# Recurrent attention with a routed expert layer: identities written by ScalarE, the elimination's first step a copy, and another order of the steps

## The chip, the cores and the metric

The kernel runs on one core of one Trainium2 chip. The metric is the device time of one execution in microseconds (us). Five engines work side by side, each through its own list of instructions in a fixed order: TensorE (PE; its weight loads are shown as PEld), VectorE (DVE), ScalarE (ACT), GpSimd (POOL) and SyncE (SP), which issues most of the transfers.

## What is computed

For each of 4 x 8 pairs of batch and head a state of 40 x 40 runs through 768 steps; its outputs are the rows that a layer of eight experts then takes:

```
for t in range(S):
    y[:, :, t] = einsum('bhd,bhde->bhe', rt, state)
    Sa = einsum('bhde,bhe->bhd', state, at)
    state = state * wt[:, :, None, :] - einsum('bhd,bhe->bhde', Sa, bt) + einsum('bhd,bhe->bhde', vt, kt)
x = y.transpose(0, 2, 1, 3).reshape(B * S, H * D)
...
out[i] = gate_w[i] * (relu(x[i] @ w1[e]) @ w2[e])      # e = argmax(x[i] @ w_gate), up to capacity rows an expert
```

## The kernel before

The sequence is cut into six tiles of 128 steps (index i), each of two chunks of 64 (c); two pairs of batches (pr) are worked side by side. For every tile: the decays are scanned and multiplied in (`scan_g`, `scan_p`, `mul_a`, `mul_kb`, VectorE); products of a and k or b go to PSUM (`kk`, `nn`, `iden`, TensorE) and are taken out (`take_kk` L408, `take_nn` L413, `take_iden`); a triangular matrix of 32 x 32 blocks is inverted on VectorE, and its blocks joined by TensorE and ScalarE (`inverse` L451); then the state goes through the chunks (`chain` L591), and the finished tile is gated and routed (`gate` L772, `route`). After the last tile the experts run (`expert` L1219, `weights` L1172), TensorE's matmuls mostly.

The inverse. `begin2` (L557) transposes `ns` into `xu`, one instruction of VectorE at L559. `nu` begins as 32 x 32 identities in each of 128 partitions: `units` (L553) takes the one `nu` buffer and `unit_` (L455) writes it on GpSimd, a memset (L457) and an affine select (L458). `elim(s)` (L470) then runs for s = 0 to 30 (to 14 in the first tile, where `nb` is 2): a multiply into `tmp` (L474), an add into `nu` (L476), each needing the one before. `back_a` (L481, instruction L483) and `back_b` (L485, L488) transpose the result back. There is one `ns`, one `xu` and one `nu`, so a tile's inverse begins after the previous one is joined: `take_a` (L531) of the second pair gives back `ns` and `nu`, `take_b` (L546) `xu`. `take_nn` writes `ns` (L54) and so stands ahead of `begin2`.

The masks. `masked` (L308) writes a product with its upper part zeroed, in one of two ways: ScalarE copies it out of PSUM (L311) and GpSimd selects in place, one half of the partitions after the other (L313); or VectorE multiplies it by a mask straight from PSUM (L317). `take_kk` uses it for `tm` (128 x 512), `take_m` (L703) for `vu` (128 x 1024), 24 times each.

The order. No step is issued where it stands in the code. `steps` (L67) records each with the engines and times that it is charged ("A.62 G1.5&V.35|V.69" is ScalarE 0.62 us, then GpSimd 1.5 us with VectorE held 0.35 us; or VectorE 0.69 us), its needs and its buffers. `order` (L88) replays all steps against clocks of the engines and lists them by when each could start, plus numbers by the step's name (`LATER`); of two ways it takes the one that ends first, the second with an added `alt` by kind (L182). `emit` issues the list, so every engine gets one fixed order, and an engine that waits at one instruction starts none behind it.

Of the kernel before, what the change touches and what calls it, by code (L numbers as in the profile page):

```python
# [19 lines left out]
P = 128  # L20
# [197 lines left out]
def scan_part(tc, keep, one, psum, w, a, kb, rv, vt, w_gate, wge, xd, lg, ident, up, SX, route, fill):  # L218
    nc = tc.nc
    V, A, G, TT = nc.vector, nc.scalar, nc.gpsimd, nc.tensor  # L220
# [3 lines left out]
    NQ = 2 * NI  # L224
    R = 104

    MU = 0.010321064
    O_TAIL = 0.00439068
    O_BIAS = 100
    GT = 44.0  # L230
    HC = 22.0
# [14 lines left out]
    free_ = {}  # L246
    for name, n in BUFS.items():
        sh, dt = SHAPE[name]
        pool = psum if name in ("pp", "p1") else keep if name in KEEP else one
        free_[name] = [pool.tile(sh, dt, name=f"{name}_{m}") for m in range(n)]  # L250
    LATER = {"chain": -1.1056, "comb": -0.6234, "decay": 0.0108, "decay_k": 0.6751, "fill": -93.3939,
             "gate": -0.2551, "gatf": 0.5712, "gatg": 0.0866, "h_": -87.8256, "hand_a": -95.2783,
             "hand_gx": -47.4258, "hand_kb": 32.6619, "hand_ns": -92.1286, "hand_nt": 48.4284, "hand_nu": -177.9352,
             "hand_px": -69.5935, "hand_rv": -128.1429, "hand_vT": -108.2623, "hand_vu": -1.3988,
             "hand_xu": -72.0023, "hand_z": -96.5145, "iden": -0.0389, "inverse": -0.0296, "inverse_": -116.0423,
             "join": -1.8911, "kk": 0.5138, "load_a": -8.3487, "load_g": -31.4497, "load_kb": -11.0853,
             "load_rv": -4.2772, "load_v": 3.2931, "load_w": -13.7808, "lower": -130.5284, "nn": -0.8242,
             "o_": -27.2877, "out": -0.0553, "p": 0.8687, "route": -0.5454, "routf": -1.663, "routg": -28.0939,
             "turn": -0.6375, "uT": 0.4697, "unit": -13.7726, "w": -26.1758, "w_": -0.1048, "x": -90.2429,
             "x_": -60.6701, "zz": 0.8588}  # L260
    sch = Schedule(nc, free_, MU, O_TAIL, O_BIAS, (0.549717, 1.23637, 1.47727), LATER)
    get, put, steps, PLAN, queue = sch.get, sch.put, sch.steps, sch.plan, sch.queue
    engine, copy, scale, dma = sch.engine, sch.copy, sch.scale, sch.dma

# [115 lines left out]
    def unit(T, c, G_):  # L380
# [61 lines left out]
        add(take_nn, "A.62 A.4 A.4|V.69 V.45 V.45", free=["pp"], needs=[("ns", i)], gives=("nn", n))  # L442
        add = steps(f"kk{pr}")
        add(kk, "P1.0", needs=[("a", nT), ("kb", nT)], take=["p1"])
        add(take_kk, "A.62 G1.5&V.35|V.69", take=["tm"], free=["p1"], gives=("tm", n))
        add = steps(f"iden{pr}")
        add(iden, "P.5", needs=[("kb", nT), ("nn", n), ("tm", n)], take=["pp"], free=["kb"] * c)
        add(take_iden, "A.46 A.46", take=["bk"], free=["pp"], gives=("bk", n))
# [2 lines left out]
    def inverse(i, G_, Ts):  # L451
        s_ = {}
        steps("inverse_0")(lambda: G_.update(ns=get("ns")), "", take=["ns"], gives=("ns", i))

        def unit_():  # L455
            nu = s_["nu"][:, 0:32]
            G.memset(nu, 0.0)  # L457
            G.affine_select(nu, nu, pattern=[[1, 32], [-1, 32]], compare_op=ALU.not_equal,  # L458
                            fill=1.0, base=0, channel_multiplier=0)

        nb = 2 if i in SIX else 1
        ne = 32 // nb
# [1 line left out]
        def diag(x):  # L464
            x = x.rearrange("p t s -> p (t s)")
            if nb == 1:
                return x[:, None, 0:1024].rearrange("p b (t s) -> p b t s", s=32)
            return x.rearrange("p (b y) -> p b y", b=2)[:, :, 0:512].rearrange("p b (t s) -> p b t s", s=32)

        def elim(s):  # L470
            n, m = ne - 1 - s, s + 1
            xu, nu = diag(s_["xu"]), diag(s_["nu"])
            tv = tmp[:, 0:nb * n * m].rearrange("p (b t j) -> p b t j", b=nb, t=n)
            V.tensor_mul(tv, xu[:, :, s + 1:ne, s:s + 1].to_broadcast([P, nb, n, m]),  # L474
                         nu[:, :, s:s + 1, 0:m].to_broadcast([P, nb, n, m]))
            V.tensor_add(nu[:, :, s + 1:ne, 0:m], nu[:, :, s + 1:ne, 0:m], tv)  # L476
# [81 lines left out]
            s_["xu"] = get("xu")  # L558
            V.transpose(square(s_["xu"]), G_["ns"][:, :, 0:32].rearrange("p u t -> p t u"))  # L559

        steps("unit")(units, "G2.3", take=["nu"], gives=("unit", i))
        add = steps("inverse")
        add(begin2, "V1.97", needs=[("nn", (pr, 2 * i + c)) for pr in range(2) for c in range(2)] + [("unit", i)], take=["xu"])
        for s in range(ne - 1):
            add(lambda s=s: elim(s), f"V{(nb * (ne - 1 - s) * (s + 1) + 190) / 960 * 2:.3f}")
        if nb == 1:
            add(back_a, "V1.94", gives=("ntd", 0, i))
            add(lambda: back_b(0, 1), "V1.22", gives=("n1", 0, i))
# [22 lines left out]
    def chain(T, U, Tn):  # L591
# [166 lines left out]
            more(take_turn, "A.33 A.33|V.33 V.33", take=["Sd"], free=["p1"], gives=("Sd", n))  # L758
        more = steps(f"out{pr}")
        more(mT, "P1.5", needs=[("uT", n), ("load_rv", (pr, i))], take=["pp"], free=["vT"])  # L760
        more(take_m, "A1.0 G2.6&V.7|V1.22", free=["pp"])
        more(yy, "P2.2" if q else "P1.4", needs=[("bk", n)] + [("Sd", n)] * (q > 0), take=["pp"],
             free=["bk", "vu"] + ["Sd"] * (q > 0) + ["rv"] * c)
        if q < NQ - 1:
# [7 lines left out]
    def gate(T):  # L772
        pr, i = T["pr"], T["i"]
        n = (pr, i)
        Q = {}

        def turn_y():
            p = Q["pt"] = get("pp")
            for h in range(H):
                TT.transpose(p[:, h // 4, h % 4 * P:h % 4 * P + R], T["px"][0:R, h, 0:P], ident[0:R, 0:R])  # L780

        def logits():
            p = Q["pt"]
# [12 lines left out]
        def x_lo():
            for x in range(2):
                V.tensor_sub(Q["x16"][:, x, 1, 0:HD].rearrange("p (h d) -> p h d", d=D), hv(x),
                             Q["x16"][:, x, 0, 0:HD].rearrange("p (h d) -> p h d", d=D))
            put("pp", Q["pt"])  # L800

        def x_rest():
            y = Q["x16"]
            copy(y[:, :, 1, HD:], y[:, :, 0, 2 * P:HD])
            copy(y[:, :, 0, HD:], y[:, :, 1, 2 * P:HD])

        def take_logits():
            t = pr * NI + i
            scale(lg[:, t::2 * NI, :], Q["pt"][:, 0, R:R + 16].rearrange("p (x e) -> p x e", x=2), 1.0 / SX)

        def store_x():
            for x in range(2):
                t = (pr + 2 * x) * NI + i
                dma(xd[i == NI - 1][t * P:(t + 1) * P, :], Q["x16"][:, x].rearrange("p a c -> p (a c)"))
            put("x16", Q["x16"])

        add = steps(f"gat{late(i)}{pr}")
        add(turn_y, "P1.0", needs=[("y", (pr, 2 * i)), ("y", (pr, 2 * i + 1))], take=["pp"])
        add(logits, "P1.6", needs=[("wge", 0)], free=["px"])
        add(take_logits, "A.2|V.2", gives=("logits", n))  # L820
        add(x_hi, "A.46 A.46|V.49 V.49", take=["x16"])
        add(x_lo, "V.49 V.49", free=["pp"])
        add(x_rest, "A.3 A.3|G.3 G.3")
        add(store_x, "L0>.55&L0>.55", needs=[("fill", 0)], free=["x16"], gives=("store_x", n))

    Ts = {}
# [610 lines left out]
```

## Time and profile before

| what | value |
|---|---|
| median of 3 runs | 695.71 us |
| lowest and highest run | 692.19 and 697.31 us |
| the profiled execution, its own time | 689.67 us |
| its span, from the first to the last instruction | 687.7 us |
| granted TensorE clock, mean | 0.884 |

The profiled execution is one more run with a recorder. All durations here come from it. Busy time of an engine is the time in which it executes; between two instructions that depend on each other a few tens of ns pass that count as idle. The granted clock is a share of full speed: 1.0 is 2.4 GHz, 0.5 is 1.2 GHz.

### The profile page before, as it was taken

Reading aid. Unit: us, or ns where it says so; the run is one execution under the profiler, and the core shown is the slowest. Engines: PE = TensorE matmul, PEld = TensorE weight load, DVE = VectorE, ACT = ScalarE, POOL = GpSimd, SP = SyncE. Lnnn points to the kernel's source line nnn. Section 1 sums busy time; section 2 is a strip of 40 time slices with the busy share of each in tenths; the row PEclk is TensorE's granted clock in tenths of the full one; section 3 lists DMA queues with packets and bytes.
Section 4 is the critical chain, followed back from the end, with each engine's and each line's share of the span. In section 5 each row is a group of like instructions: output and inputs, shape, how many; then the busy total and the mean of one; then the engine's idle time right before and its main releaser. Section 6 shows DMA issues by size and latency. Waiting matters only on the chain.

```text
span 687.7 us, 25344 instructions
## 1 busy us (share of the span) xinstructions
PE 559.8 (81%) x11268; PEld 438.9 (64%) x11268; DVE 444.3 (65%) x832; ACT 292.8 (43%) x569; POOL 196.8 (29%) x260
## 2 busy tenths in 40 slices
PE   0627788888878898788889866979998999999991
PEld 0626677877767788677778865736753556556471
DVE  7997899979995898798778754442424635344210
ACT  8603654535623455343553443332524534443320
POOL 8400321342222204420420024222371234241121
PEclk9955998879968987798988878979999999999997
DMA  7770043311521253034011337612789956857000
GB/s 191 209 168 4 5 108 98 102 34 55 163 83 56 80 125 95 18 97 132 27 34 37 107 103 180 151 52 67 219 157 285 217 121 173 226 118 190 24 30 13
DMA packets 72683, 74.78 MB, mean 109 GB/s; under 512 B 37644, under 2 KB 61326, under 8 KB 71604
## 3 DMA queue, kind: packets, MB, share of 16 engines
q1 hardware_dynamic: 68308, 63.08, 34.9%
q0 software_dynamic: 4256, 9.99, 5.0%
q8 instruction: 90, 1.47, 0.9%
q14 instruction: 29, 0.24, 0.1%
HBM read 57.46 MB, written 10.65 MB: 99 GB/s over the span
## 4 chain that ended last, share of the span: by engine, by line
issue 27%; PE 24%; DVE 22%; POOL 9%; ACT 7%; DMA 5%; another core or an unknown queue 2%; SPq 1%; POOLq 0%; DVEq 0%; ACTq 0%
PE pp L269 13%; DVE tmp L474 7%; DVE nu L476 7%; PE p L269 6%; POOL out_dram L1151 5%; POOL a L1124 2%; PE pp L646 2%; DVE vu L317 2%; ACT ns L54 2%; DMA px<-in_moe_w_dram 1%; DMA a<-in_a_dram 1%; POOL vT L1124 1%; PE pp L780 1%; DVE xu L559 1%
## 5 line engine op out<-in xcount | busy, mean ns | idle before, releaser
L476 DVE TENSOR_TENSOR nu<-nu,tmp 128x31 f32<-128x31 f32 (+20 forms) x170 | 69.5, 409 | 5.9
L1151 POOL DMA_INDIRECT out_dram<-tm,ri x32 | 33.1, 1035 | 133.1 <-ACT tm L1295 124.9
L474 DVE TENSOR_TENSOR tmp<-xu,nu 128x31 f32<-128x31 f32 (+20 forms) x170 | 67.4, 396 | 4.7
L313 POOL TENSOR_SCALAR_AFFINE_SELECT tm<-tm 64x512 f32<-64x512 f32 x46 | 33.1, 719 | 109.7 <-ACT tm L311 90.3
L269 PE MATMUL pp<-vu,bk 128*40 128x128 f32 (+1 forms) x768 | 52.5, 298 | 5.1 <-POOL vu L313 2.9
L269 PEld LDWEIGHTS pp<-vu,bk 128*40 128x40 f32 x768 | 45.1, 131 | 9.6 <-POOL vu L313 3.3
L1267 PE MATMUL pp<-xT,kb 128*128 128x480 f16 (+2 forms) x192 | 43.5, 328 | 0.8 <-DVE vT L1275 0.8
L269 PE MATMUL pp<-a,kb 64*64 64x64 f32 x768 | 22.1, 255 | 26.8 <-DVE a L364 17.3
L1295 ACT ACTIVATE tm<-p,gs 128x320 f32<-128x320 f32 (+1 forms) x32 | 16.8, 525 | 57.3 <-PE p L1146 31.9
L1015 POOL DMA_INDIRECT meta<-mt,sloti x24 | 27.2, 1135 | 45.4 <-DVE tmp L474 15.0
L269 PE MATMUL p<-nu,ns 64*32 64x32 f32 (+1 forms) x1024 | 21.6, 210 | 21.2 <-DVE nu L488 17.5
L269 PEld LDWEIGHTS pp<-a,kb 64*64 64x64 f32 x768 | 18.1, 161 | 28.8 <-issue 22.7
L435 ACT ACTIVATE bk<-pp,sgn 128x320 f32<-128x320 f32 x48 | 22.7, 532 | 32.1 <-PE pp L269 28.9
L269 PE MATMUL pp<-rv,vT 64*64 64x64 f32 x1536 | 32.8, 239 | 4.1 <-ACT vT L50 2.1
L317 DVE TENSOR_TENSOR vu<-pp,mask 128x1024 f32<-128x1024 f32 x16 | 19.5, 1222 | 24.7 <-PE pp L269 21.2
L1267 PE MATMUL pp<-xT,px 128*128 128x480 f16 (+2 forms) x128 | 35.0, 328 | 0.1
L269 PE MATMUL pp<-zs,nt 64*64 64x40 f32 x768 | 19.2, 251 | 18.9 <-ACT zs L50 17.5
L269 PEld LDWEIGHTS p<-nu,ns 64*32 64x32 f32 (+1 forms) x1024 | 20.0, 132 | 22.6 <-issue 16.9
L269 PEld LDWEIGHTS pp<-rv,vT 64*64 64x64 f32 x1536 | 29.2, 151 | 7.8 <-ACT vT L50 4.5
L269 PE MATMUL p<-a,kb 64*64 64x64 f32 x768 | 33.4, 250 | 0.7 <-ACT tm L311 0.4
L457 POOL MEMSET nu<- 128x1024 f32 x6 | 5.7, 954 | 98.0 <-PE p L269 98.0
L1146 PEld LDWEIGHTS <-nt 128*128 128x128 f16 (+1 forms) x256 | 25.2, 102 | 12.8 <-issue 1.9
(222 smaller groups left out, 1458.5 us busy)
## 6 DMA issues: line engine op xcount, KB each, us to landing
vu<-in_moe_w_dram SPq DMA_DIRECT2D x32, 320.0 KB
kb<-in_kb_dram SPq DMA_DIRECT2D x24, 320.0 KB
px<-in_w_dram SPq DMA_DIRECT2D x12, 512.0 KB
vu<-in_vt_dram SPq DMA_DIRECT2D x48, 128.0 KB
px<-in_moe_w_dram SPq DMA_DIRECT2D x12, 512.0 KB
xd<-x SPq DMA_DIRECT2D x24, 192.0 KB
a<-in_a_dram SPq DMA_DIRECT2D x24, 160.0 KB
rv<-in_rv_dram SPq DMA_DIRECT2D x24, 160.0 KB
```

The costliest lines, as they stand in the source:

```text
L269: TT.matmul(out, l, r, start=start, stop=True, skip_group_check=True)
L313: G.affine_select(out[half(x)], out[half(x)], pattern=[[0, n] for n in sh[1:-1]] + [[1, C]], compare_op=ALU.is_gt, fill=0.0, base=0, chann ...
L317: V.tensor_mul(out, in_, m.to_broadcast(sh))
L435: A.activation(U["bk"][:, x].rearrange("p h d -> p (h d)"), U["pi"][:, x, 0:HD], AF.Copy, scale=sgn[:, x:x + 1])
L474: V.tensor_mul(tv, xu[:, :, s + 1:ne, s:s + 1].to_broadcast([P, nb, n, m]), nu[:, :, s:s + 1, 0:m].to_broadcast([P, nb, n, m]))
L476: V.tensor_add(nu[:, :, s + 1:ne, 0:m], nu[:, :, s + 1:ne, 0:m], tv)
L1015: nc.gpsimd.indirect_dma_start(out=meta_v[t][:, :], out_offset=bass.IndirectOffsetOnAxis(ap=su[:, t:t + 1], axis=0), in_=mt[:, t, :], in_o ...
L1124: nc.gpsimd.indirect_dma_start(out=xt(j)[:c].rearrange("p a c -> p (a c)"), out_offset=None, in_=src[:, :], in_offset=bass.IndirectOffsetO ...
L1146: nc.tensor.matmul(po[:, :DM], h[l], rr(f, 1)[:, 0], start=(f == 0 and m == 0), stop=(f == NF - 1 and m == 2))
L1151: nc.gpsimd.indirect_dma_start(out=out_v[used[0] % (8 * E)][:, :], out_offset=bass.IndirectOffsetOnAxis(ap=ri.bitcast(U32)[:c, j, 1:2], ax ...
L1267: nc.tensor.matmul(s_["h", f + z][:, :n], l, rr, start=m % 7 == 0 and m < 14, stop=m >= 14)
L1295: nc.scalar.activation(ob[:c], s_["o", j][:c, :DM], AF.Copy, scale=s_["gs"][:c, j:j + 1])
```

## The change

`unit_` no longer uses GpSimd: ScalarE writes 1024 zeros a partition (`ident` scaled by 0.0) and copies ones onto every 33rd element. With s = 0 `elim` copies a column of `xu` into `nu`, as `nu` holds the identity there. The charges of some steps are altered: VectorE is no longer charged beside GpSimd's selects. `LATER` and three other numbers of the order are new, so the whole list of steps is.

```
-    MU = 0.010321064
+    MU = 0.0092889579
...
-    LATER = {"chain": -1.1056, "comb": -0.6234, "decay": 0.0108, "decay_k": 0.6751, "fill": -93.3939,
+    LATER = {"chain": -0.2976, "comb": -5.1223, "decay": 0.0469, "decay_k": 0.7249, "fill": -97.222, "gate": -0.2551,
...
-    sch = Schedule(nc, free_, MU, O_TAIL, O_BIAS, (0.549717, 1.23637, 1.47727), LATER)
+    sch = Schedule(nc, free_, MU, O_TAIL, O_BIAS, (1.42109, 1.49794, -0.061783), LATER)
...
+    ones = one.tile([P, 1], F32, name="ones")
+    G.memset(ones, 1.0)
...
-        add(take_kk, "A.62 G1.5&V.35|V.69", take=["tm"], free=["p1"], gives=("tm", n))
+        add(take_kk, "A.62 G1.45|V.69", take=["tm"], free=["p1"], gives=("tm", n))
...
         def unit_():
-            nu = s_["nu"][:, 0:32]
-            G.memset(nu, 0.0)
-            G.affine_select(nu, nu, pattern=[[1, 32], [-1, 32]], compare_op=ALU.not_equal,
-                            fill=1.0, base=0, channel_multiplier=0)
+            nu = s_["nu"][:, 0:32].rearrange("p t s -> p (t s)")
+            A.activation(nu.rearrange("p (m t) -> p m t", t=P), ident[:, None, :].to_broadcast([P, 8, P]), AF.Copy, scale=0.0)
+            A.copy(nu[:, ::33], ones.to_broadcast([P, 32]))
...
             xu, nu = diag(s_["xu"]), diag(s_["nu"])
+            if s == 0:
+                V.tensor_copy(nu[:, :, 1:ne, 0:1], xu[:, :, 1:ne, 0:1])
+                return
...
-        steps("unit")(units, "G2.3", take=["nu"], gives=("unit", i))
+        steps("unit")(units, "A1.02 A.26", take=["nu"], gives=("unit", i))
...
-            add(lambda s=s: elim(s), f"V{(nb * (ne - 1 - s) * (s + 1) + 190) / 960 * 2:.3f}")
+            add(lambda s=s: elim(s), f"V{(nb * (ne - 1 - s) * (s + 1) + 160) / 960 * 2:.3f}")
...
-        more(take_m, "A1.0 G2.6&V.7|V1.22", free=["pp"])
+        more(take_m, "A1.0 G2.4|V1.22", free=["pp"])
...
-        add(x_rest, "A.3 A.3|G.3 G.3")
+        add(x_rest, "A.3 A.3|G.76 G.76")
```

What the new numbers choose, counted over the whole list: of the 24 masks of `vu`, ScalarE and GpSimd made 8 (16 selects) and VectorE 16; now VectorE makes all 24. Of the 24 of `tm`, VectorE made 1 and now makes 3; GpSimd's selects of `tm` go from 46 to 42. VectorE takes over 6 copies into `vu` (64 x 320), 4 casts of `x` (128 x 320) and 1 copy of `vT` (128 x 1024) from ScalarE, and gives it 4 copies of `Sd`, one `take_nn` of three instructions, and two small ones. GpSimd takes over 2 copies of `x`. The matmuls and their number stay.

GpSimd, from the first tile's `tm` masks through the second tile. Before:

```order
L980 MEMSET empty 128x192
L457 MEMSET nu_119 128x1024
L458 AFFINE_SELECT nu_119<-nu_119 128x1024
L313 AFFINE_SELECT tm_113<-tm_113 64x512 x2
L313 AFFINE_SELECT tm_115<-tm_115 64x512 x2
L313 AFFINE_SELECT vu_132<-vu_132 64x1024 x2
L313 AFFINE_SELECT tm_114<-tm_114 64x512 x2
L313 AFFINE_SELECT tm_116<-tm_116 64x512 x2
L313 AFFINE_SELECT vu_131<-vu_131 64x1024 x2
L313 AFFINE_SELECT vu_133<-vu_133 64x1024 x2
```

The same place now:

```order
L983 MEMSET empty 128x192
L314 AFFINE_SELECT tm_114<-tm_114 64x512 x2
L314 AFFINE_SELECT tm_115<-tm_115 64x512 x2
L314 AFFINE_SELECT tm_116<-tm_116 64x512 x2
L50 COPY x_0_142<-x_0_142 128x2x64 x4
```

The identity and three masks of `vu` are gone from it, and one mask of `tm`.

VectorE in the middle of the second tile's elimination (tmp and nu are its two alternating instructions). Before:

```order
L476 TENSOR_TENSOR nu_119<-nu_119,tmp 128x24x8
L317 TENSOR_TENSOR vu_130<-pp_93,mask 128x1024
L474 TENSOR_TENSOR tmp<-xu_118,nu_119 128x207
L476 TENSOR_TENSOR nu_119<-nu_119,tmp 128x23x9
L675 COPY D_145<-pp_93 104x8x40
L474 TENSOR_TENSOR tmp<-xu_118,nu_119 128x220
```

The beginning of the same elimination now, and behind it the place of those rows:

```order
L562 STREAM_TRANSPOSE xu_118<-ns_117 128x1024
L474 COPY nu_119<-xu_118 128x31
L318 TENSOR_TENSOR vu_130<-pp_95,mask 128x1024
L477 TENSOR_TENSOR tmp<-xu_118,nu_119 128x60
L479 TENSOR_TENSOR nu_119<-nu_119,tmp 128x30x2
...
L479 TENSOR_TENSOR nu_119<-nu_119,tmp 128x23x9
L318 TENSOR_TENSOR vu_132<-pp_94,mask 128x1024
L477 TENSOR_TENSOR tmp<-xu_118,nu_119 128x220
```

The first step is one copy, and four masks of `vu` stand within this elimination where one stood.

ScalarE where the second tile's inverse has been joined (qq and nt) and the next tile's `ns` is filled. Before:

```order
L50 COPY qq_124<-p_1_97 128x512
L54 ACTIVATE ns_117<-pp_93,neg 128x512
L54 ACTIVATE ns_117<-pp_93 32x8x32 x2
L50 COPY nt_123<-p_0_96 32x16x32 x2
L54 ACTIVATE ns_117<-pp_95,neg 128x512
L54 ACTIVATE ns_117<-pp_95 32x8x32 x2
```

The same place now:

```order
L50 COPY qq_124<-p_0_96 128x512
L458 ACTIVATE nu_119<-ident 128x1024
L459 COPY nu_119<-ones 128x32
L50 COPY nt_123<-p_1_97 32x16x32 x2
L54 ACTIVATE ns_117<-pp_93,neg 128x512
L54 ACTIVATE ns_117<-pp_93 32x8x32 x2
```

Two instructions more stand between `qq` and the first `ns`; it is so in each of the five later tiles.

## Rows read from the trace of the kernel before

**Rows 1.** Stretches: length; busy PE, PEld, DVE, ACT, POOL; PEclk, DMA share, GB/s.

```profile
74.00:112.00 38.00, 31.18 (x912) 27.34 (x912) 35.47 (x70) 17.89 (x34) 12.51 (x14) 0.96 0.23 60
112.00:176.00 64.00, 55.73 (x1586) 50.03 (x1586) 57.10 (x118) 32.13 (x70) 17.69 (x19) 0.87 0.29 83
176.00:247.00 71.00, 58.30 (x1590) 52.73 (x1591) 58.03 (x118) 30.13 (x67) 16.46 (x19) 0.83 0.29 88
247.00:317.00 70.00, 58.37 (x1599) 52.95 (x1597) 60.90 (x120) 32.52 (x68) 21.54 (x23) 0.85 0.33 91
317.00:390.00 73.00, 63.69 (x1787) 57.13 (x1788) 58.94 (x121) 32.96 (x71) 13.92 (x19) 0.88 0.17 48
390.00:445.00 55.00, 43.27 (x1105) 37.81 (x1100) 26.60 (x52) 22.93 (x41) 17.71 (x22) 0.81 0.56 148
445.00:688.00 243.00, 216.65 (x1397) 130.39 (x1395) 86.74 (x153) 87.34 (x163) 72.42 (x86) 0.95 0.53 136
```

**Rows 2.** Timeline of VectorE, second tile's elimination: start us, us, instruction.

```profile
101.14 0.36 DVE L474 TENSOR_TENSOR tmp<-xu,nu 128x192 f32<-128x192 f32 x1
101.53 1.17 DVE L476 TENSOR_TENSOR nu<-nu,tmp 128x192 f32<-128x192 f32 x1
...
105.14 1.14 DVE L474 TENSOR_TENSOR tmp<-xu,nu 128x156 f32<-128x156 f32 x1
106.31 0.32 DVE L476 TENSOR_TENSOR nu<-nu,tmp 128x156 f32<-128x156 f32 x1
```

**Rows 3.** Timeline of GpSimd in the same stretch.

```profile
101.36 4.75 POOL L313 TENSOR_SCALAR_AFFINE_SELECT vu<-vu 64x1024 f32<-64x1024 f32 x4 [2.16 <-ACT vu L311]
```

**Rows 4.** Instructions of line 313: count, duration ns min/median/max.

```profile
L313 POOL TENSOR_SCALAR_AFFINE_SELECT tm<-tm x46: 649/658/2558, 23.3 to 371.7; 64x512 f32<-64x512 f32 x46
...
L313 POOL TENSOR_SCALAR_AFFINE_SELECT vu<-vu x16: 1137/1144/1178, 82.8 to 352.9; 64x1024 f32<-64x1024 f32 x16
```

**Rows 5.** Timeline of VectorE in the first tile.

```profile
15.01 2.21 DVE L364 TENSOR_TENSOR a<-a,px 104x1024 f32<-104x1024 f32 x1
...
21.85 1.22 DVE L364 TENSOR_TENSOR a<-a,px 104x1024 f32<-104x1024 f32 x1
```

**Rows 6.** Instructions on nu, as rows 4.

```profile
L458 POOL TENSOR_SCALAR_AFFINE_SELECT nu<-nu x6: 1267/1776/3364, 13.0 to 331.1; 128x1024 f32<-128x1024 f32 x6
```

**Rows 7.** Line 317, as rows 4, and what VectorE waited for ahead of it (us, times).

```profile
L317 DVE TENSOR_TENSOR vu<-pp,mask x16: 1212/1225/1225, 82.1 to 436.2; 128x1024 f32<-128x1024 f32 x16
...
  PE pp L269: 21.2, 6
```

**Rows 8.** Timeline of VectorE about the second tile's begin2.

```profile
68.61 0.17 DVE L357 COPY g<-gx 104x8 f32<-104x8 f32 x1
...
73.85 1.97 DVE L559 STREAM_TRANSPOSE xu<-ns 128x1024 f32<-128x1024 f32 x1 [1.80 <-ACT ns L54]
75.92 0.20 DVE L474 TENSOR_TENSOR tmp<-xu,nu 128x31 f32<-128x31 f32 x1
76.23 0.21 DVE L476 TENSOR_TENSOR nu<-nu,tmp 128x31 f32<-128x31 f32 x1
```

**Rows 9.** Costliest groups of VectorE to 450 us, shapes apart: busy us, mean ns.

```profile
L50 DVE CAST x<-pp 128x320 f16<-128x320 f32 x2 | 0.9, 478 | 0.0
```

**Rows 10.** Timeline of ScalarE ahead of the same begin2.

```profile
72.34 0.69 ACT L54 ACTIVATE ns<-pp,neg 128x512 f32<-128x512 f32 x1
73.06 0.76 ACT L54 ACTIVATE ns<-pp 32x256 f32<-32x256 f32 x2
```

**Rows 11.** Groups of ScalarE to 450 us, as rows 9.

```profile
L286 ACT COPY kb<-tmp 128x1024 f32<-128x1024 f32 x4 | 4.0, 1042 | 0.0
...
L54 ACT ACTIVATE lg<-pp 128x16 f32<-128x16 f32 x7 | 1.3, 182 | 4.3 <-PE pp L269 4.2
```

**Rows 12.** Waits to 450 us: who for whom, us in total, times, longest.

```profile
PE p L269 <- DVE nu L488: 17.5, 5, 13.0
...
DVE xu L559 <- ACT ns L54: 2.5, 3, 1.8
```

More of the change, by code (lines that the diff above doesn't have):

```diff
@@ L225, in scan_part @@
     R = 104
-    MU = 0.010321064
-    O_TAIL = 0.00439068
+    MU = 0.0092889579
+    O_TAIL = 0.004451612
     O_BIAS = 100
@@ L250, in scan_part @@
         free_[name] = [pool.tile(sh, dt, name=f"{name}_{m}") for m in range(n)]
-    LATER = {"chain": -1.1056, "comb": -0.6234, "decay": 0.0108, "decay_k": 0.6751, "fill": -93.3939,
[L252 to L260, printed above, removed]
-    sch = Schedule(nc, free_, MU, O_TAIL, O_BIAS, (0.549717, 1.23637, 1.47727), LATER)
+    LATER = {"chain": -0.2976, "comb": -5.1223, "decay": 0.0469, "decay_k": 0.7249, "fill": -97.222, "gate": -0.2551,
+             "gatf": 0.7144, "gatg": -2.3618, "h_": -93.7763, "hand_a": -103.7075, "hand_gx": -46.3284,
+             "hand_kb": 39.4252, "hand_ns": -103.3447, "hand_nt": 56.0046, "hand_nu": -170.23, "hand_px": -58.0583,
+             "hand_rv": -125.6083, "hand_vT": -100.5399, "hand_vu": 10.8513, "hand_xu": -75.1102, "hand_z": -73.262,
+             "iden": 0.1938, "inverse": 0.2486, "inverse_": -98.6045, "join": -3.8145, "kk": 0.5138,
+             "load_a": -10.1403, "load_g": -0.6507, "load_kb": -9.543, "load_rv": -0.1776, "load_v": 0.8939,
+             "load_w": -11.6091, "lower": -139.6835, "nn": -0.826, "o_": -0.3199, "out": -0.0527, "p": 0.8101,
+             "route": 0.2922, "routf": -0.2962, "routg": -24.8644, "turn": -0.703, "uT": 0.4697, "unit": -9.3836,
+             "w": -20.1216, "w_": 0.8755, "x": -104.8416, "x_": -62.5388, "zz": 0.4931}
+    sch = Schedule(nc, free_, MU, O_TAIL, O_BIAS, (1.42109, 1.49794, -0.061783), LATER)
     get, put, steps, PLAN, queue = sch.get, sch.put, sch.steps, sch.plan, sch.queue
```

## The prediction

> **What bounds the kernel now.** I read the busy time by stretch first [rows 1]. The kernel has two parts. From 445 us to the end the experts run, and TensorE is busy 216.65 of 243 us: nothing in this change removes work from it there, so I take that stretch, and the way into it from 390 us, as it is, only beginning earlier or later. The five stretches from 74 to 390 us are the tiles. There VectorE is busy 35.47 + 57.10 + 58.03 + 60.90 + 58.94 = 270.4 of 316 us and TensorE 267.3 (the same rows): two engines almost equally long, neither of them full. In the first of these stretches VectorE has 35.47 of 38 us.
>
> Next I read the timeline of one elimination, since each of its instructions needs the one before. An add of 192 elements a partition takes 1.17 us where the multiply of the same shape just ahead took 0.36; a multiply of 156 takes 1.14 where the add of that shape behind it takes 0.32 [rows 2]. GpSimd runs four selects on `vu` in just this stretch, 4.75 us in all [rows 3]. So a select on GpSimd lengthens an instruction of VectorE by 1.17 - 0.36 = 0.81 or 1.14 - 0.32 = 0.82 us. A multiply by the decays from SBUF shows it too: 2.21 us at 15.01, where the identity's select runs (it begins at 13.0 [rows 6]), and 1.22 without one [rows 5]: 0.99 us. The mask that VectorE makes straight from PSUM isn't lengthened by any: its shortest and longest are 1.212 and 1.225 us [rows 7]. So VectorE pays for GpSimd's work within a chain that cannot be reordered. That is what the change touches.
>
> **The change, term by term.** All sums are against the profiled execution, 689.67 us; the median of the runs is 695.71, 6.0 us above it, and I carry the difference over to the median. A measurement of this kernel can tell about 1% from no change, which is 7 us.
>
> (a) The 16 selects of `vu` [rows 4] go. At 0.81 us each on VectorE that is 13.0 us. Some may have fallen beside work that can't be held; as a lower bound I take half, 6.5.
>
> (b) The six selects of the identity [rows 6] go. At 0.81 to 0.99 us each: 4.9 to 5.9, I take 5.4 us. GpSimd's own time isn't counted: it was busy 82 of the 316 us [rows 1].
>
> The Trainium skill, "SBUF — State Buffer", section "Who interferes with whom", says that a VectorE instruction with two SBUF inputs contends with a GpSimd one that reads SBUF, that the loser is blocked for all of the other's instruction, and that an instruction with one SBUF input outside the two-port modes is free. The trace agrees on who is held (0.36 to 1.17 us, against the mask's 1.225), but not on all of the length: by that rule the 16 selects would cost 16 x 1.144 = 18.3 us, and (a) would be 5 us larger.
>
> (c) VectorE gets 8 masks of `vu` at 1.22 us [rows 7]: +9.8 us.
>
> (d) The first step of six eliminations is a copy in place of 0.20 and 0.21 us [rows 8]. No copy of that shape is in the trace; the small copy of 8 elements takes 0.17 [rows 8]. I take 0.20, so 0.21 plus some hand-over is saved, six times: -1.4 us. Bounds: 0 and -2.
>
> The same page says that fp32 copies from SBUF to SBUF can use two ports and then contend with GpSimd, which speaks against a copy here. At worst it would meet a select of `tm` each time, 6 x 0.66 us = 4 us more.
>
> (e) Two more masks of `tm` go to VectorE, at half of (c)'s price: +1.2 us; four selects of `tm` go, and with a select of half the length [rows 4] I take half of 0.81 for each: -1.6. Sum -0.4.
>
> (f) VectorE takes 10 copies and casts of 0.48 us [rows 9] and one copy of 1.2 us (priced as a mask of that size [rows 7]): +6.0. It gives away 4 copies of `Sd`, three instructions of `take_nn` and two small ones: nine at some 0.4 us, -3.6. Sum +2.4.
>
> VectorE together: -13.0 - 5.4 + 9.8 - 1.4 - 0.4 + 2.4 = -8.0 us, in a chain that I take to be the longer of the two.
>
> (g) ScalarE gets the identity: 1.04 us as a copy of that size from SBUF [rows 11], and for the 32 ones 0.18 as its smallest instruction on data [rows 11], I take 0.25 for the stride: 1.29 us, and 0.4 to 1.5 as bounds. Queued behind it are the last `nt`, the `ns` and with them `begin2`, for which VectorE waits, and behind that all of its elimination. Where ScalarE was the last to come this counts in full: the second tile, where VectorE waited 1.80 us for `ns` [rows 8], and where ScalarE also gets the fourth `take_nn`, 0.69 + 0.76 us [rows 10]. That is +2.7 us. In the other tiles the waits for `ns` were 2.5 - 1.8 = 0.7 us together [rows 12], and ScalarE is busy less than half of each stretch [rows 1], so there I count 0. If all five paid, it would be 5 x 1.29 + 1.45 = 7.9.
>
> (h) The order. Before, a pair of selects was charged to VectorE at 0.7 us for `vu` and 0.35 for `tm`, and the identity at nothing. The trace has some 1.6 a pair for `vu`; 8 x 0.92 and the identity's 5.4 are 12.8 us of VectorE that the list didn't know, 2.6 a tile. A list that runs late on one engine makes the others wait in the wrong places: TensorE waited 17.5 us in five for the last transpose of the inverse [rows 12], VectorE 21.2 us in six for TensorE ahead of a mask [rows 7]. With VectorE on its times some of both goes. No row tells how much; the bounds are 0 or a loss of the same size (another list can be worse), and 17.5. I take a quarter of 17.5, -4.5 us, as the lag explains 2.6 of the 3.5 us a tile and not all of it will be found again.
>
> Sum: -8.0 + 2.7 - 4.5 = -9.8 us. That is 679.9 for the profiled execution and 695.7 - 9.8 = 685.9 for the median. What is late next in the tiles is TensorE: its 267.3 us are now the longer row.
>
> **Rivals.** *TensorE takes over.* If VectorE's stretch falls from 270.4 to 262.4 while TensorE's stays at 267.3, only 3.1 us of the 8.0 reach the end; with (g) and no gain from the order that is -0.4: 695 us. For it: the two rows are so near. Against it: TensorE's time is part of the same alternation (it waited 17.5 us for VectorE), and its granted clock of 0.83 to 0.88 in the four long stretches [rows 1] shows that part of its busy time is at half clock, which fewer waits would shorten.
>
> *The masks bring their waits along.* VectorE takes its instructions in order, so a mask that comes before TensorE's product holds the whole elimination behind it. In the trace six of 16 masks waited, 3.5 us each [rows 7]. Four masks now stand in the second tile's elimination, one of them straight behind the first step. If each of the 8 new ones waits 3.5 us, that is 28 us, and the time 685.9 + 28 = 714. It decides from 9.8 / 8 = 1.2 us a mask, where the gain is gone, and from 2.1 the kernel is slower by over 1%. Against it: 10 of 16 did not wait, and the new list charges the masks with the 1.22 us that they take.
>
> *The order gives more.* If all of the 17.5 us goes, the sum is -8.0 + 2.7 - 17.5 = -22.8: 673.
>
> That the stalls stay though the change is made I leave out: 26 of the 68 selects that made them are no longer in the list. What stays are those of `tm`, 42 at some 0.4 us, 17 us at most.
>
> **How the numbers follow.** I give the forecast 0.44, the better order 0.15, TensorE as the bound 0.27 and the masks' waits 0.14. The first two are faster by over 1% (under 688.8) but for a small part: 0.58. The third is within 1%, with some of the forecast's upper edge and of the masks' small waits: 0.30. Slower is the rest of the masks' case: 0.12. The range reaches from the better order, 673 less some for (a) by the longer price, so 671, past TensorE's 695 to waits of 1.5 us a mask, 698; the forecast's own range is 679 to 692.
>
> **What would show it.** VectorE's instructions in the eliminations should show no 1.1 us rows, only some of 0.7 beside selects of `tm`. Busy VectorE in the tiles should fall by some 8 us, and the last elimination's `back_a` should end some 10 us earlier, with the stretch from there to the end as long as before. (g) is right if VectorE waits longer for `ns` in the second tile alone. I am wrong if VectorE's waits ahead of masks add up to more than 31 us, or if the last `back_a` is earlier and the end isn't: then the way into the experts sets it.

## The result, and the profile after

The changed kernel takes 686.28 us, the median of 20 runs (675.42 to 696.04); 20 runs of the kernel before, beside it, have a median of 693.00 (685.26 to 704.82). The ratio is 0.988, with a 95% interval of 0.984 to 0.992. Forecast were 685.9 us, 9.8 less than the 695.71 of the three runs it started from; beside the 20 runs the kernel is 6.7 us faster, so a third of the forecast's 9.8 did not come, and the medians still meet because the starting point was too high by nearly as much, 2.7 us. That is luck. A ratio is taken here from each kernel's runs near its fastest one, a median from all of its runs. The profiled execution took 683.09 us, its span 681.1, with a mean granted clock of 0.890; before these were 689.67, 687.7 and 0.884.

On two other chips, in the experiments below, the same kernel was no faster than the one before: 0.5% slower by the ratios, 0.2 and 0.3% by the medians. The number was right on the first chip; that the reasoning behind it made it so is not shown.

First the stretches of the changed kernel (same columns as [rows 1]):

```profile
74.00:112.00 38.00, 33.11 (x902) 29.31 (x902) 30.85 (x65) 16.00 (x35) 4.33 (x7) 0.96 0.38 97
112.00:176.00 64.00, 56.19 (x1740) 50.52 (x1734) 58.65 (x107) 30.23 (x65) 11.95 (x12) 0.95 0.30 96
176.00:247.00 71.00, 53.69 (x1459) 48.53 (x1460) 60.76 (x127) 30.48 (x62) 12.52 (x15) 0.78 0.30 76
247.00:317.00 70.00, 60.79 (x1826) 54.68 (x1828) 62.40 (x136) 35.60 (x77) 11.52 (x17) 0.92 0.32 89
317.00:390.00 73.00, 60.64 (x1822) 54.75 (x1818) 54.51 (x118) 31.62 (x66) 11.00 (x17) 0.85 0.17 52
```

From 74 to 390 us VectorE is busy 267.2 us where it was 270.4, TensorE 264.4 where it was 267.3. GpSimd falls most, from 82 to 51 us. By stretches of fixed length work slides across the edges; over the whole span VectorE went from 444.3 to 437.0 us, 7.3 less.

Next the timeline of VectorE at the start of the second tile's elimination, and a little later (columns as in [rows 2]; the bracket is the idle time before and who ended it):

```profile
75.70 2.02 DVE L562 STREAM_TRANSPOSE xu<-ns 128x1024 f32<-128x1024 f32 x1 [1.97 <-ACT ns L54]
77.76 0.61 DVE L474 COPY nu<-xu 128x31 f32<-128x31 f32 x1
78.27 1.21 DVE L318 TENSOR_TENSOR vu<-pp,mask 128x1024 f32<-128x1024 f32 x1
...
82.55 0.49 DVE L678 COPY D<-pp 104x320 f32<-104x320 f32 x1 [1.51 <-PE pp L268]
...
85.69 0.36 DVE L477 TENSOR_TENSOR tmp<-xu,nu 128x192 f32<-128x192 f32 x1
86.08 0.36 DVE L479 TENSOR_TENSOR nu<-nu,tmp 128x192 f32<-128x192 f32 x1
...
91.44 0.49 DVE L678 COPY E<-pp 104x320 f32<-104x320 f32 x1 [1.10 <-PE pp L268]
...
95.69 0.91 DVE L479 TENSOR_TENSOR nu<-nu,tmp 128x252 f32<-128x252 f32 x1
96.63 0.75 DVE L477 TENSOR_TENSOR tmp<-xu,nu 128x255 f32<-128x255 f32 x1
97.42 0.42 DVE L479 TENSOR_TENSOR nu<-nu,tmp 128x255 f32<-128x255 f32 x1
...
113.04 0.49 DVE L673 TENSOR_TENSOR E<-pp,g 104x320 f32<-104x320 f32 x1 [2.23 <-PE pp L268]
```

The add of 192 elements that took 1.17 us [rows 2] takes 0.36. What is still lengthened stands beside a select of `tm`: 0.91 and 0.75 against 0.42. The pauses for TensorE have grown: 1.51, 1.10 and 2.23 us at 82.55, 91.44 and 113.04, 4.8 us within this chain. The kernel before also had other work of VectorE in it, one mask, these copies into D and E and two multiplies of `px`, but only one pause for TensorE:

```profile
89.14 0.49 DVE L675 COPY E<-pp 104x320 f32<-104x320 f32 x1 [0.33 <-PE pp L269]
```

The instructions by line (columns as in [rows 4, 7]):

```profile
L318 DVE TENSOR_TENSOR vu<-pp,mask x24: 1198/1217/1225, 78.3 to 426.1; 128x1024 f32<-128x1024 f32 x24
...
L318 DVE TENSOR_TENSOR tm<-p,mask x3: 660/665/673, 73.1 to 331.0; 128x512 f32<-128x512 f32 x3
```

```profile
L458 ACT ACTIVATE nu<-ident x6: 1052/1060/1061, 15.4 to 320.4; 128x1024 f32<-128x1024 f32 x6
...
L459 ACT COPY nu<-ones x6: 246/248/249, 16.6 to 321.5; 128x32 f32<-128x32 f32 x6
```

And the waits to 450 us (columns as in [rows 12]):

```profile
PE p L268 <- DVE nu L491: 22.9, 6, 10.3
...
DVE vu L318 <- PE pp L268: 16.2, 8, 5.7
...
DVE D L676 <- remote: 9.4, 2, 6.0
...
ACT ns L54 <- remote: 5.3, 1, 5.3
```

VectorE's waits ahead of the masks fell from 21.2 us in six [rows 7] to 16.2 in eight, though there are 24 masks now and not 16. TensorE's waits for the inverse's last transpose grew, from 17.5 us [rows 12] to 22.9. "Remote" is a wait whose releaser the trace doesn't show; more on it below.

Where the time came from: the last `back_a` starts at 377.17 us, 9.3 earlier than at 386.50. From there to the end it is 303.9 us, where it was 301.2. So 6.6 us of span are won, all of them in the tiles and some given back behind them. In the terms of VectorE's own time, up to the start of that `back_a` (length; busy; clock, DMA share, GB/s), before and changed:

```profile
0.00:386.50 386.50, 327.52 (x625) 0.85 0.31 87
```

```profile
0.00:377.17 377.17, 318.44 (x613) 0.87 0.33 89
```

It is busy 9.1 us less and idle as long as before (59.0 and 58.7 us). In this pair of profiles the last `back_a` is earlier by nearly what VectorE's work fell. That is an account of two traces and no proof of a cause; the second chip below shows a like fall, 7.4 us, without a gain in the medians.

### The profile page after: what moved, and what is told of

The parts are those of the page before. It is cut to its first block, busy times and chain, and to the rows that moved or that the text cites. A ratio compares the mean times of both kernels' runs of the same rounds, so it can differ in the third digit from the quotient of the medians.

```text
span 681.1 us, 25336 instructions
## 1 busy us (share of the span) xinstructions
PE 556.4 (82%) x11268; PEld 436.4 (64%) x11268; DVE 437.0 (64%) x838; ACT 291.1 (43%) x567; POOL 153.5 (23%) x231
## 4 chain that ended last, share of the span: by engine, by line
issue 33%; PE 28%; DVE 21%; POOL 8%; ACT 4%; DMA 2%; SPq 1%; another core or an unknown queue 0%; POOLq 0%; DVEq 0%; ACTq 0%
PE pp L268 17%; PE p L268 6%; POOL out_dram L1154 4%; DVE tmp L477 4%; DVE nu L479 4%; PE pp L649 2%; POOL a L1127 2%; DVE gx L351 2%; DVE px L360 2%; DVE kb L371 2%; DVE vu L318 2%; ACT ns L54 1%; DVE xu L486 1%; DMA kb<-in_kb_dram 1%; PE pp L428 1%
## 5 line engine op out<-in xcount | busy, mean ns | idle before, releaser
L479 DVE TENSOR_TENSOR nu<-nu,tmp 128x87 f32<-128x87 f32 (+12 forms) x164 | 60.1, 367 | 5.6
L477 DVE TENSOR_TENSOR tmp<-xu,nu 128x87 f32<-128x87 f32 (+12 forms) x164 | 59.3, 361 | 4.2
L1270 PE MATMUL pp<-xT,kb 128*128 128x480 f16 (+5 forms) x256 | 48.9, 325 | 0.0
L268 PE MATMUL p<-nu,ns 64*32 64x32 f32 (+1 forms) x1024 | 25.1, 223 | 26.1 <-DVE nu L491 22.9
L50 POOL COPY x<-x 128x128 f16<-128x128 f16 x18 | 13.0, 720 | 139.4 <-ACT x L50 51.6
L1298 ACT ACTIVATE tm<-p,gs 128x320 f32<-128x320 f32 (+1 forms) x32 | 16.8, 526 | 61.4 <-PE p L1149 31.8
L268 PEld LDWEIGHTS pp<-rv,vT 64*64 64x64 f32 x1536 | 29.0, 139 | 18.6 <-issue 12.8
L268 PEld LDWEIGHTS p<-nu,ns 64*32 64x32 f32 (+1 forms) x1024 | 23.2, 144 | 27.2 <-DVE nu L491 22.3
L318 DVE TENSOR_TENSOR vu<-pp,mask 128x1024 f32<-128x1024 f32 x24 | 29.0, 1216 | 16.2 <-PE pp L268 16.2
L268 PEld LDWEIGHTS pp<-a,kb 64*64 64x64 f32 x768 | 19.5, 175 | 25.4 <-ACT a L285 14.7
L1278 DVE SCALAR_TENSOR_TENSOR rv<-pp,px 128x480 f16<-128x480 f32 (+2 forms) x20 | 10.3, 559 | 38.7 <-ACT px L1275 37.0
L1018 POOL DMA_INDIRECT meta<-mt,sloti x24 | 24.0, 999 | 44.6 <-DVE mt L1015 31.6
L268 PEld LDWEIGHTS p<-a,kb 64*64 64x64 f32 x768 | 30.0, 158 | 4.4 <-issue 2.7
```

Source lines behind the costliest of these rows:

```text
L268: TT.matmul(out, l, r, start=start, stop=True, skip_group_check=True)
L318: V.tensor_mul(out, in_, m.to_broadcast(sh))
L1018: nc.gpsimd.indirect_dma_start(out=meta_v[t][:, :], out_offset=bass.IndirectOffsetOnAxis(ap=su[:, t:t + 1], axis=0), in_=mt[:, t, :], in_o ...
L1270: nc.tensor.matmul(s_["h", f + z][:, :n], l, rr, start=m % 7 == 0 and m < 14, stop=m >= 14)
L1298: nc.scalar.activation(ob[:c], s_["o", j][:c, :DM], AF.Copy, scale=s_["gs"][:c, j:j + 1])
```

## The experiments

One sum is used throughout. For each instruction of VectorE I take how much longer it was than the shortest of its line and shape, and leave out differences of under some 0.05 us; where GpSimd ran beside it, that is what the prediction called the lengthening. It was 30.6 us in the kernel before (12.8 beside selects of `vu`, 11.5 beside those of `tm`, 5.3 beside the identity) and 11.2 in the changed one (10.4 beside `tm`). The three groups of runs were made on three chips, each with its own runs of the kernel before beside it. That the first pair ran on a fourth one is inferred from its times; the number of that chip is not on record.

### The edits alone, with the list of before (first group)

Beside these runs the kernel before had a median of 667.28 us (35 runs). The first kernel takes only `unit_` from the change, with the tile `ones` that it reads (calls shortened):

```
-            G.memset(nu, 0.0)
-            G.affine_select(nu, nu, ...)
+            A.activation(nu..., ident..., AF.Copy, scale=0.0)
+            A.copy(nu[:, ::33], ones.to_broadcast([P, 32]))
```

> The list of before, word for word; only the identity is written by ScalarE at its old place in the list. If the selects on GpSimd hold VectorE and VectorE is on the path, six stalls of 0.81 to 0.99 us go (5.4 us) and ScalarE's 1.3 us is paid once, in the second tile: 4 us faster than before (ratio 0.994). If the tiles are bound elsewhere: no change (1.000). If ScalarE's 1.3 us is paid in every tile: 1 us faster (0.998).

Measured: 669.8 us, ratio 1.0021 (0.9980 to 1.0062). The lengthening beside the identity is gone (22.9 us in all is left), and the time isn't. By the prediction's prices this edit alone was worth 5.4 us less 1.3 on ScalarE, a ratio of 0.994, which is outside the interval. Part of the reason may lie in its waits to 450 us: ahead of `begin2` VectorE waited 2.5 us for `ns` in the kernel before [rows 12] (2.4 on the second group's chip, 3.1 in the next kernel, both with GpSimd's identity), and here 5.2.

```profile
DVE xu L560 <- ACT ns L54: 5.2, 4, 3.6
```

So in this list ScalarE's identity lengthened that waiting by 2 to 3 us, not by 1.3. The 5.3 us of relief less that would still have been a gain of some 3 us, 0.996, which the interval doesn't hold either.

The second makes every mask of `vu` on VectorE, at the place where the list of before puts ScalarE's copy:

```
-        if queue[1] == "A":
+        if queue[1] == "A" and len(sh) == 3 and sh[1] == H:
```

> The list of before; only the 8 masks of vu that ScalarE and GpSimd made are made by VectorE, at their old place. If the stalls are the cost: 16 x 0.81 us of stalls go and 8 x 1.22 us come, 3 us faster (0.995). If the masks bring their waits for TensorE along at 3.5 us each, 25 us slower (1.036); at the mean over all masks of before, 1.3 us each, 7 us slower (1.010).

Measured: 665.5 us, 0.9982 (0.9940 to 1.0024). The lengthening falls to 16.8 us, none of it beside `vu`. By price it was worth -13.0 + 9.8 = -3.2 us, 0.995; the interval holds that and zero.

The third is both, and the copy as the first step:

```
+            if s == 0:
+                V.tensor_copy(nu[:, :, 1:ne, 0:1], xu[:, :, 1:ne, 0:1])
+                return
```

> The list of before with all edits of the bodies: identity by ScalarE, first step a copy, the 8 masks by VectorE. If the edits alone make the gain: 5.4 + 3.2 + 1.4 - 1.3 = 8.7 us faster than before (0.987), as fast as the changed kernel or faster. If the new list makes half of it, as forecast: 4 to 5 us faster (0.993). If the new list makes all of it: 1.000.

Measured: 664.56 us, 0.9984 (0.9939 to 1.0028). The lengthening is 11.9 us, near the changed kernel's, and the three edits together change the time by -1.1 us, from -4.1 to +1.9 by the interval (-2.7 by the medians). The prediction's prices for these edits, (a) to (d) and 1.3 us of (g), are -8.7 us: 0.987, outside.

The fourth is the changed kernel with `unit_` written by GpSimd again (the first diff the other way round):

> The changed kernel and its list, with the identity written by GpSimd again (memset and select). By the stalls: 5.4 us come back, ScalarE's 1.3 us in the second tile goes: 4 us slower than the changed kernel (ratio to before 0.994 in place of 0.988). If the identity's place was of no account: as fast as the changed kernel (0.988).

Measured: 677.3 us, 1.0129 (1.0087 to 1.0170). The lengthening is 15.9 us, 3.8 of it beside the identity. With the new list and nearly all of the relief the kernel is slower here than the one before. That the new list brings the gain of the first chip was in doubt from here on. The changed kernel itself was not run on this chip. On the two others its ratio is 1.005, so GpSimd's identity seems to cost the new list some 0.75%, 5 us, where 4 were expected; across chips that is a hint and no proof. It would mean that the same edit is worth its price in one list and nothing in the other.

### Lengthening added on purpose (second group)

Another chip; the kernel before has 672.05 us there (29 runs). Its profile, for comparison:

> The kernel before, unaltered, on the chip of this group, for its rows. On the chip of the first four runs it took 667.3 us where the first pair of traces came from one at 693.0. If TensorE's instructions came late on the first chip, the rows here have no wait for nothing that the profile shows, in the middle of a group of matmuls, of the kind seen at 203 to 209 us, and the tiles end some 15 us earlier with the same busy times.

The profiled run took 681.14 us, more than any of the 29, so it tells of durations and of kinds of wait, and little of arrival times: its last `back_a` starts at 380.6 us, 5.9 earlier than on the first chip and not some 15. The lengthening is 27.8 us, against 30.6 there. VectorE's wait ahead of its masks is 7.7 us in five there, where it was 21.2 in six [rows 7]:

```profile
PE p L269 <- DVE nu L488: 17.4, 4, 13.0
...
DVE vu L317 <- PE pp L269: 7.7, 5, 2.7
...
DVE vu L317 <- remote: 1.1, 1, 1.1
```

The changed kernel beside it, unaltered:

> The changed kernel, unaltered, on the chip of this group. If its gain is of the work on VectorE, the ratio is 0.988 here too. If it hangs on a chip on which TensorE's instructions come late, or on the chance of the order, the ratio is 1.00 on a chip as fast as that of the first four runs, where the old list with all edits had 0.998 and the new list with GpSimd's identity 1.013.

Measured: 673.27 us, 1.0054 (1.0011 to 1.0098). The gain of the first chip isn't there. The lengthening is 10.7 us, against 11.2 in its first trace. VectorE's time up to the last `back_a`, for the kernel before and this one:

```profile
0.00:380.63 380.63, 325.08 (x625) 0.84 0.32 88
```

```profile
0.00:367.74 367.74, 317.66 (x613) 0.89 0.34 91
```

VectorE is busy 7.4 us less here too, and the last `back_a` of these two profiles lies 12.9 us apart, while the medians are level. The profiled runs, 681.14 and 667.14 us, lie above all 29 runs of the one kernel and at the lowest of the other: one profile of each says little of a few microseconds. The waits of the changed kernel:

```profile
PE p L268 <- DVE nu L491: 22.3, 7, 10.7
...
DVE vu L318 <- PE pp L268: 5.7, 9, 1.9
```

The next two add 84 instructions of GpSimd behind the selects of `tm`, on a tile that nothing else uses; one kernel selects, the other only writes:

```
+    spare = one.tile([P, 7, 32], F32, name="spare")
...
+            for x in (0, 0, 1, 1):
+                G.affine_select(spare[half(x)], spare[half(x)], pattern=[[0, 7], [1, 32]], ...)
```

```
+            for x in (0, 0, 1, 1):
+                G.memset(spare[half(x)], 0.0)
```

> The changed kernel with four more selects of 64 x 224 on a spare tile behind each of the 21 pairs of tm selects, 84 in all, some 31 us of GpSimd's time and nothing that another engine needs. Selects of tm now lengthen VectorE by 10.4 us in 27.5 us of selects, so these should add some 12 us to VectorE's busy time. If VectorE bounds the tiles: 10 us slower than the changed kernel. If TensorE has taken over, as the first four runs suggest: 3 us or less.

> The same with memsets of 64 x 224 in place of the selects: GpSimd writes and reads nothing. If it is GpSimd's reading that holds VectorE, its busy time is that of the changed kernel and the time too (within 2 us). If any work on GpSimd does it, as slow as with the selects, in proportion to its time there.

Measured: 674.26 us, 1.0047 (1.0014 to 1.0079) with the selects, 671.29 us, 1.0014 (0.9978 to 1.0050) with the memsets. Timelines of GpSimd and VectorE, first with selects:

```profile
92.60 2.12 POOL L319 TENSOR_SCALAR_AFFINE_SELECT spare<-spare 64x224 f32<-64x224 f32 x4
...
93.07 0.37 DVE L482 TENSOR_TENSOR tmp<-xu,nu 128x220 f32<-128x220 f32 x1
93.48 0.46 DVE L484 TENSOR_TENSOR nu<-nu,tmp 128x220 f32<-128x220 f32 x1
93.97 0.48 DVE L482 TENSOR_TENSOR tmp<-xu,nu 128x231 f32<-128x231 f32 x1
```

and with memsets:

```profile
95.67 0.75 DVE L481 TENSOR_TENSOR tmp<-xu,nu 128x255 f32<-128x255 f32 x1
...
96.20 1.27 POOL L319 MEMSET spare<- 64x224 f32 x4
...
96.45 0.42 DVE L483 TENSOR_TENSOR nu<-nu,tmp 128x255 f32<-128x255 f32 x1
```

The add of 220 elements takes 0.46 us beside selects, 0.39 elsewhere; that of 255 takes 0.42 beside memsets, its usual time. Over the kernel the selects add 6.6 us of lengthening, about half of the 12 expected (15.4 in all, since those beside `tm` fell to 7.9), and the memsets none (11.2 in all). The memsets are shorter, 0.28 us against 0.41, and might be too short to hold anything. That is answered by the identity's memset of 0.95 us in the profile of the kernel before on this chip; an instruction of VectorE with both inputs in SBUF that runs wholly within it takes 0.19 us, as all six of its kind do:

```profile
329.71 0.95 POOL L457 MEMSET nu<- 128x1024 f32 x1 [24.08 <-PE p L269]
...
330.35 0.19 DVE L1004 TENSOR_TENSOR oh<-eidx,ix 128x32 f32<-128x32 f32 x1
```

So it is GpSimd's reading that holds VectorE. The Trainium skill, "SBUF — State Buffer", section "Who interferes with whom", says so of a VectorE instruction with two SBUF inputs, and these runs agree. What the lengthening costs at the end is less clear. The kernel with selects has 4.7 us more of it than the unaltered one and is 1.0 us slower by the medians; it has 4.2 us more than the one with memsets, which gives GpSimd as many instructions, and is 3.0 us slower. All the intervals overlap. Anything from nothing to nearly the full price fits.

### Both lists on one chip, and one list for each half (third group)

A third chip; the kernel before has 668.78 us (29 runs). First the changed kernel, then the list of before with the three edits:

> The changed kernel on a third chip, beside the three that follow. If the gain of the first chip belongs to the change, the ratio to before is 0.988; if the second chip's result is the rule, 1.005. VectorE's begin2 of the third tile is expected at 144 us and the last back_a at 368 to 377 us.

> The list of before with all three edits of the body (identity by ScalarE, copy as the first step, masks of vu by VectorE). If the new list brings the gain, this one is slower than the changed kernel beside it by some 5 us or more; if the two lists are worth the same, the ratios differ by under 0.5%. begin2 of the third tile at 137 us, from there to the last back_a 233 us.

Measured: the changed kernel 670.47 us, 1.0052 (1.0013 to 1.0092), as on the second chip; the old list with the edits 671.4 us, median of 12 runs. Its ratio, 0.9953 (0.9885 to 1.0021), rests on its three lowest runs, one of which stands alone 6 us under the next; by medians it is 1.004. By the medians the two lists are 0.9 us apart, by the ratios 1%: a difference between them is not shown. Their eliminations, from the start of each `begin2` to that of its `back_a`, us:

| tile | before, first chip | changed, first chip | changed, third chip | old list and edits, third chip |
|---|---|---|---|---|
| 1 | 29.2 to 41.8 | 31.5 to 43.6 | 31.5 to 43.7 | 28.3 to 40.4 |
| 2 | 73.9 to 109.5 | 75.7 to 116.1 | 77.3 to 119.0 | 73.8 to 108.3 |
| 3 | 133.7 to 172.5 | 143.7 to 178.4 | 146.4 to 182.7 | 138.6 to 175.5 |
| 4 | 199.3 to 244.5 | 203.5 to 243.8 | 207.2 to 243.9 | 201.4 to 239.5 |
| 5 | 275.3 to 315.5 | 269.1 to 310.5 | 270.9 to 312.8 | 270.4 to 308.6 |
| 6 | 350.3 to 386.5 | 339.6 to 377.2 | 338.8 to 374.4 | 338.6 to 372.5 |
| sum of tiles 2 to 6 | 196 | 194 | 192 | 182 |
| sum of the four pauses between them | 117 | 107 | 105 | 117 |

The new list shortens the four pauses by 12 us (105 against 117 on the third chip) and lengthens the five eliminations by 10 (192 against 182): it puts other work, four masks in the second tile among it, inside the chain. Its second tile also begins 3.5 us later (77.3 against 73.8).

To see whether the early loss and the later gain can be parted, the list was made with one set of numbers (`MU`, `O_TAIL`, the three `alt`, `LATER` and the charges) up to 125 us of the planner's own clock (about the third `begin2`), and with the other behind it:

```
+    sch.phases, sch.change = (OLD, NEW), 125.0
...
+            ph = int(clock["V"] >= self.change)
```

> All edits of the body; the list is made with before's numbers and charges up to 125 us of the planner's clock (the third tile's begin2), then with the changed ones. Theory: the new list loses 7 us in the first two tiles (144.5 against 137.5 us to that begin2) and wins 10 in the later ones (223 against 233). Then begin2 comes at 137, the last back_a near 361, and the kernel is 7 us faster than the changed one, 1.0%. Rival: what the new list does late it has already paid for early (work taken ahead), so this one is within 0.5% of the changed one or of the old list.

> The other way round: the changed numbers up to 125 us of the planner's clock, before's behind it, all edits of the body. Theory: early loss without the later gain, begin2 at 144, the last back_a near 377, some 7 to 10 us slower than the changed one. Rival as there: within 0.5% of the others, as the work taken ahead comes back.

Measured: old then new 679.18 us (six runs), 1.0199 (1.0128 to 1.0269), the slowest of all; new then old 673.36 us, 1.0046 (0.9998 to 1.0094). The theory forecast 7 us less than the changed kernel for the first, which is 8.7 more by the medians, and 7 to 10 more for the second, which is 2.9 more. The rows that it spoke of, the third `begin2` and the last `back_a`, old then new:

```profile
136.78 1.94 DVE L593 STREAM_TRANSPOSE xu<-ns 128x1024 f32<-128x1024 f32 x1 [2.15 <-ACT ns L55]
...
372.63 1.91 DVE L517 STREAM_TRANSPOSE xu<-nu 128x1024 f32<-128x1024 f32 x1
```

and new then old:

```profile
144.06 1.96 DVE L593 STREAM_TRANSPOSE xu<-ns 128x1024 f32<-128x1024 f32 x1
...
370.98 1.94 DVE L517 STREAM_TRANSPOSE xu<-nu 128x1024 f32<-128x1024 f32 x1
```

The early halves do what was said (137 and 144 us). The later ones don't: with the new numbers it takes 235.9 us from there, not 223; with the old ones 226.9, not 233. It fits that whoever reaches the third tile late has more work behind it already; that was not counted. All four kernels of this chip have their last `back_a` between 371.0 and 374.4 us. (The profiled run of old then new was the lowest of its six, 672.97 us, so its trace doesn't show why the others were longer.) For these lists the time to the end of the tiles isn't a sum of halves.

## Why the prediction was right, and where it wasn't

By its terms, on the first chip:

| term | forecast, us | found |
|---|---|---|
| (a) selects of `vu` gone | -13.0 | -12.8 of lengthening, 15 instructions |
| (b) identity's selects gone | -5.4 | -5.3 |
| (c) eight more masks | +9.8 | 24 at 1.22, so +9.8 |
| (d) first step a copy | -1.4 | 0.19 in place of 0.41, six times: -1.3 (one was held to 0.61, counted under (e)) |
| (e) `tm` | -0.4 | two more masks +1.3, lengthening -1.1: +0.2 |
| (f) small copies | +2.4 | lines L50 and L54 of VectorE, 7.3 to 9.8 us: +2.6 |
| VectorE in all, (a) to (f) | -8.0 | -7.3 busy |
| (g) identity on ScalarE | +2.7 | 1.06 + 0.25 us each, as priced; ahead of the second `begin2` VectorE waits 1.97 us, where it was 1.80: +0.2 |
| (h) the order | -4.5 | TensorE's wait for the inverse +5.4, VectorE's ahead of the masks -5.0 |
| in all | -9.8 | span -6.6, median -6.7 |

Right were the prices of VectorE's instructions. The lengthening stood where it was read, two neighbouring rows of one shape gave its size, and counting instructions gave VectorE's busy time to a microsecond. The copy of the first step was held by a select of `tm` once, at 77.76: 0.61 us, where the median of the six is 0.19. The Trainium skill, "SBUF — State Buffer", section "Who interferes with whom", lets such copies from SBUF to SBUF contend, and this row agrees.

Not borne out beyond the first chip was the step "VectorE together ... -8.0 us, in a chain that I take to be the longer of the two", by which the whole of it reaches the end. On the first group's chip the relief, with the list left alone, was worth 1.1 us by the ratio and 2.7 by the medians, where 8.7 were priced. That is near the case called *TensorE takes over*, given 0.27: its -0.4 us lies within the three intervals of that group's old lists. In the old list with the edits TensorE is the longer row in the tiles (74 to 390 us; columns as in [rows 1]):

```profile
74.00:390.00 316.00, 277.23 (x7742) 250.67 (x7744) 268.86 (x574) 147.99 (x317) 53.82 (x74) 0.85 0.29 80
```

while in the changed kernel on the same chip the two are level:

```profile
74.00:390.00 316.00, 268.24 (x7848) 240.85 (x7843) 269.78 (x564) 148.07 (x313) 52.18 (x70) 0.89 0.29 81
```

The rows fit, but TensorE's granted clock differs between them too, 0.85 and 0.89; neither engine is full there, and which of the two sets the pace was not varied by itself.

The price of (g) was too low where the list stays as it was: from 2.4 to 3.1 us with GpSimd's identity the waits ahead of `begin2` rose to 5.2, 4.7 and 4.4 us in the three kernels with ScalarE's, by some 2 us for the 1.29. In the new list it is 1.1 us with GpSimd's identity and 2.0, 2.0 and 2.7 with ScalarE's, a rise of 0.9 to 1.6 us.

Wrong too was what (h) rested on. It took a quarter of the 17.5 us that TensorE waits for the inverse, and this wait grew to 22.9 (22.3 and 21.5 on the other chips; 15.5 with the old list and the edits on the third). With most of the uncharged lengthening gone the wait did not shrink. What the term overlooked is in the table of eliminations: a list can shorten the pauses and pay for it inside the chain. Nor did it look at the first tile, where the new list loads `a` ahead of `kb`. VectorE idles for that, and `begin2` comes 2.3 us later than before:

```profile
10.19 1.31 DVE L365 TENSOR_TENSOR a<-a,px 104x1024 f32<-104x1024 f32 x1
13.40 2.36 DVE L371 TENSOR_TENSOR kb<-kb,gx 104x1024 f32<-104x1024 f32 x2 [1.90 <-DMA kb<-in_kb_dram]
```

*The masks bring their waits along* did not come: 24 masks waited 16.2 us on the first chip, 5 less than 16 masks before, and 5.7 and 3.5 on the others, where this case needs 9.8 us more of it than before. What came instead are the pauses ahead of D and E inside the elimination, which no term held.

What made the first chip's 6.7 us stays open. The kernels are the same; the chip, it seems, isn't. Before took 693 us there and 667 to 672 on the others, and only there do the traces of these two kernels show long waits without a visible releaser: five to 450 us in the kernel before, 22.3 us together, and three in the changed one, 14.7, against 1.1, 0 and 0 in their three later profiles. One of them, on ScalarE and on TensorE ahead of it, in the kernel before ("issue" means that the engine waited for nothing that the profile shows):

```profile
204.26 0.33 PE L269 MATMUL pp<-E,a 64*64 64x40 f32 x4 [0.28 <-issue]
204.96 0.35 PE L269 MATMUL pp<-E,a 64*64 64x40 f32 x4 [0.38 <-issue]
205.75 0.32 PE L269 MATMUL pp<-E,a 64*64 64x40 f32 x4 [0.43 <-issue]
206.46 0.29 PE L269 MATMUL pp<-E,a 64*64 64x40 f32 x2 [0.40 <-issue]
...
208.87 0.43 ACT L50 COPY zs<-pp 128x320 f32<-128x320 f32 x1 [6.24 <-remote]
```

A row of like matmuls comes in pieces, and who waits for its product waits 6 us. A kernel might gain where TensorE comes late in this way, by keeping VectorE and TensorE less tightly coupled. The traces do not bear that out: up to the last `back_a` these waits were 12.2 us before and 8.6 in the changed kernel, but VectorE's idle time there was the same in both, 59.0 and 58.7 us. What they do show, its 9.1 us less of work, is 7.4 us on the second chip, and there the medians show no gain. So neither the relief nor the late matmuls are shown to be the cause; the first pair was not run again on its chip.

## What to carry to other kernels

A lengthened instruction can be priced to a tenth of a microsecond from two neighbouring rows, and what its removal is worth at the end is still open: here 8.7 us by price came to between 1 and 3 on one chip and to nothing clear on another. Add some of it on purpose and see what the end does, before paying for its removal, and add enough: some 4 us of it could not be told from the scatter of the runs. Where two engines alternate and each is busy five sixths of the time, take a full price for a relief on one as the best case, not the default. And a list of steps that looks better in one trace should be timed on a second chip: these two differ by -1.2% on one and +0.5% on two others (-1.0, +0.2 and +0.3% by the medians).

## What the runs showed that was not expected

- How long a select holds VectorE goes, in most rows, by its length in a simple way. A select of 1.144 us (64 x 1024) lengthens an instruction by 0.81 to 0.82 us [rows 2 to 4], one of 0.66 us (64 x 512) by 0.33 (0.75 against 0.42 above), one of 0.41 us (64 x 224) by 0.07 (0.46 against 0.39): each time its own length less some 0.33 us. Of the 28 rows beside `tm` in the changed kernel 18 lie at 0.33 to 0.38 and nine at 0.43 to 0.51, as the 0.91 against 0.42 above.
- One program differs by up to 4% between its four sets of runs, three of them on chips known to differ (before: 693, 667, 672 and 669 us), and a gain of one set can be missing in the others.
